# Linear attention ahead of a routed feed-forward layer: loads of k, v and q by head to 128 partitions, or by batch to 64

## The chip, the core and the metric

The kernel runs on one core of a Trainium2 chip. The metric is the time of one execution on the device, in microseconds (us). The kernel before has a median of 359.92 us in three runs (358.19 to 360.01). A profiled execution took 357.99 us, of which the profile shows a span of 355.7 us.

## The reference

Two layers follow each other. The first is attention without a softmax, over 8 batches, 8 heads, 576 rows and 64 numbers a row, in 32-bit floats:

```python
kv = np.einsum('bhsd,bhse->bhde', k, v)
out = np.einsum('bhsd,bhde->bhse', q, kv)
rms = np.sqrt(np.mean(out * out, axis=-1, keepdims=True) + 1e-06)
return (out / rms * g_norm).astype(np.float32)
```

So each head has one 64 x 64 matrix, k transposed times v, which needs every row of k and v; only then can a row of q be multiplied by it. The 8 heads of a row make 512 numbers, and 8 x 576 = 4608 such rows go to the second layer. It sends each row to the one of 8 experts with the largest gate value, through two matrices (512 x 1024 and 1024 x 512) with a ReLU between, and weights the result by the gate.

## The kernel before

**Attention.** The batches go in four pairs, P = 0 to 3. In an SBUF tile the first batch of a pair fills partitions 0 to 63, the second 64 to 127. Of the 576 rows of a head, the first 512 go to a main tile of 128 partitions x 8 heads x 512 numbers: partition p holds rows 8p to 8p + 7, so 8 x 64 numbers that lie together in memory, 2 KB. The last 64 rows go to a remainder tile (`load_rem`, L203), one row a partition. `load_main` (L211) brings a main tile, or some heads of it (`hs`), or some of the eight rows of each partition (`js`).

**What is loaded when.** `load_first` (L244) issues pair 0: k on SP's queue, v on ACT's, then q on SP's in two halves of `js`. All other loads are on SP's queue, in the order of the program: k, v and q of pair 1, k and v of pair 2 (L558), and then at fixed steps q of pair 2 (L506), k and v of pair 3 (L503), q of pair 3 (L507, in two halves), the weights of the first expert (L534) and of the second (L535, L536). k and v have two buffers each, for even pairs (kA, vA) and odd pairs (kB, vB, which lie in the slots of expert weights), and q has two. A load waits for its buffer's last reader. Completion is told by eight semaphores that the loads take in turn, so a load also waits for the one that had its semaphore before.

**What follows the loads.** `kv_mm` (L279) multiplies k and v of two heads for each call, four calls a pair; `kv_copy` (L297), `kv_t` and `kv_gate` prepare the result, with the gate's weights multiplied in. Then a loop of 36 steps (L574), nine for each pair, runs: a step s takes the j-th of the eight rows of every partition (or, for j = 8, the remainder tile). `heads` (L267) has POOL copy that row out of the main tile, four steps ahead; `x_qt` (L342) transposes it on PE, two steps ahead; `x_mm` (L352) multiplies; `x_norm` (L367) norms it on ACT and DVE. `Route` (L407) finds the expert and the place of each row, and `scatter` (L477) has POOL write the rows to a scratch tensor in DRAM, in the order of experts. The order on each engine is written by hand: lists `mid`, `late` and `last` (L488 to L536) say what stands behind which step. In POOL's order, the copy of `heads` for a step stands ahead of the ticks (L513, which pace POOL by DVE) and scatters of the step four earlier.

**The experts.** `gather` (L657) brings rows of one expert, five tiles of 128, with an indirect DMA from POOL; `flip` transposes them, `one` (L697) is the first matrix (L705) and ReLU (L712), `two` (L716) the second (L719), and L727 scatters the results to the output. Eight experts, and a ninth job for rows beyond 640 of an expert, follow each other. Weights come two experts ahead in 32 bits (L138, L146), to 128 partitions, and are cast (L168, L170, L175).

Of the kernel before, what the change touches and what calls it, by code (L numbers as in the profile page):

```python
# [28 lines left out]
def kernel(  # L29
# [154 lines left out]
    with (  # L184
# [6 lines left out]
        main, rem, qp, kvst, kvsb = {}, {}, {}, {}, {}  # L191
        srcs = {"k": k, "v": v, "q": q}
# [17 lines left out]

        def load_main(n, P, hs, js, eng):  # L211

            for bb in range(2):
                rows = srcs[n][2 * P + bb, hs, 0:512, :].rearrange("h (p j) d -> p h j d", j=8)
                dst = main[n, P][64 * bb:64 * bb + 64, hs, :].rearrange(
                    "p h (j d) -> p h j d", d=64
                )
                eng.dma_start(
                    dst[:, :, js, :].rearrange("p h j d -> p h (j d)"),
                    rows[:, :, js, :].rearrange("p h j d -> p h (j d)"),  # L220
                )

        ALL = slice(0, 8)
# [2 lines left out]
        def load_kv(P):  # L226
            for n in "kv":
                new_main(n, P)
                load_rem(n, P, nc.sync)
            for hs in HALF:  # L230
                for n in "kv":
                    load_main(n, P, hs, ALL, nc.sync)

        def load_q(P):
            new_main("q", P)
            if P == 3:
                load_main("q", P, ALL, HALF[0], nc.sync)
                load_rem("q", P, nc.sync)
                load_main("q", P, ALL, HALF[1], nc.sync)
            else:  # L240
                load_main("q", P, ALL, ALL, nc.sync)
                load_rem("q", P, nc.sync)
# [608 lines left out]
```

## Time and profile before

| What | Value |
|---|---|
| time, median of three | 359.92 us |
| span in the profile | 355.7 us |
| PE busy (matmul) | 271.1 us, 76% |
| DVE, ACT, POOL busy | 157.0, 159.0, 152.7 us |
| SP's queue (q1) | 39968 packets, 63.92 MB |
| indirect DMAs of POOL (q0) | 6976 packets, 18.96 MB |
| ACT's queue (q10) | 2880 packets, 2.38 MB |
| k, v, q main loads, size of one DMA | 512 or 1024 KB |

A row of slices cuts the span into 40 equal parts; a digit is the busy share in tenths. "GB/s" is what the core's 16 DMA engines moved in the slice. A row of waits reads: engine, tile and line that waited, what it waited for, then us in total, times, and the longest. A queue's row has packets, MB and the time that its packets took, as a share of 16 engines over the window that was asked; packets overlap in part, so a share can pass 100%. A row of the timeline starts with the time and the length of one or several equal instructions.

### The profile page before, as it was taken

What the parts mean: (1) busy time and instruction counts of PE and PEld (TensorE: products, weight loads), DVE (VectorE), ACT (ScalarE), POOL (GpSimd) and SP (SyncE); (2) the same over time, 40 slices, a digit from 0 to 9 for tenths busy, and PEclk for the clock granted to TensorE, in tenths of its full rate; (3) what the DMA queues carried; (4) which work ended last, traced back from release to release, by engine and by line L of the source; (5) the groups of instructions that cost most, each with busy time, mean ns of one, the idle gap of its engine ahead of it and who ended that gap; (6) DMA issues with size and microseconds to landing.
All of it is one profiled execution on the core that took longest, in us unless ns stands there. A gap on an engine that the chain in (4) does not pass through costs nothing. (4 is left out here: it accounts for less than half of the span.)

```text
span 355.7 us, 8916 instructions
## 1 busy us (share of the span) xinstructions
PE 271.1 (76%) x3684; PEld 180.5 (51%) x3684; DVE 157.0 (44%) x411; ACT 159.0 (45%) x338; POOL 152.7 (43%) x206
## 2 busy tenths in 40 slices
PE   7088725486653963676636999999999999999994
PEld 2056514474552753564412655656575747474742
DVE  0000532148612582448781239654545546363431
ACT  1001622156312552446577432737474747465652
POOL 8002200046216253256575753765555747413233
PEclk9678978779868597879658899999999999999998
DMA  7998999999999999994122792799798989896712
GB/s 150 223 218 185 200 228 226 214 210 249 254 217 221 258 246 293 377 381 169 67 99 74 254 361 81 274 308 398 237 400 260 363 284 383 262 394 202 282 61 83
DMA packets 49864, 85.82 MB, mean 241 GB/s; under 512 B 16797, under 2 KB 21150, under 8 KB 49824
## 3 DMA queue, kind: packets, MB, share of 16 engines
q1 hardware_dynamic: 39968, 63.92, 65.0%
q0 software_dynamic: 6976, 18.96, 15.1%
q10 hardware_dynamic: 2880, 2.38, 3.4%
q8 instruction: 29, 0.48, 0.6%
q14 instruction: 11, 0.09, 0.1%
HBM read 71.71 MB, written 15.50 MB: 245 GB/s over the span
## 5 line engine op out<-in xcount | busy, mean ns | idle before, releaser
L712 ACT ACTIVATE ht<-hp 128x320 f16<-128x320 f32 (+1 forms) x136 | 57.9, 428 | 71.5 <-PE hp L705 57.0
L705 PE MATMUL hp<-xt,we 128*128 128x320 f16 (+1 forms) x544 | 79.8, 295 | 0.0
L719 PE MATMUL yp<-we,ht 128*128 128x512 f16 x328 | 72.3, 379 | 0.0
L727 POOL DMA_INDIRECT out_dram<-ys,idx x41 | 42.6, 1038 | 64.9 <-DVE ys L724 56.6
L705 PEld LDWEIGHTS <-we 128*128 128x128 f16 x544 | 50.6, 98 | 19.1 <-issue 0.6
L361 PE MATMUL op<-kvs,qts 64*64 64x72 f32 x1152 | 34.8, 264 | 29.1 <-issue 18.7
L724 DVE TENSOR_SCALAR ys<-yp,xe 128x512 f32<-128x512 f32 x41 | 30.6, 750 | 47.1 <-PE yp L719 47.1
L719 PEld LDWEIGHTS <-ht 128*128 128x128 f16 x328 | 32.1, 98 | 37.1
L386 DVE TENSOR_REDUCE ms<-sq 128x8 f32<-128x512 f32 x36 | 24.5, 680 | 56.6 <-ACT sq L381 56.6
L275 POOL COPY qp<-qm 128x512 f32<-128x512 f32 x32 | 19.0, 614 | 70.5 <-DMA qm<-in_q_dram 70.5
L658 POOL DMA_INDIRECT xe<-xs_scratch,rowi x40 | 40.5, 1013 | 14.4 <-issue 9.6
L361 PEld LDWEIGHTS op<-kvs,qts 64*64 64x64 f32 x1152 | 28.7, 165 | 35.4 <-issue 20.6
L381 ACT ACTIVATE sq<-op 128x512 f32<-128x512 f32 x36 | 21.2, 590 | 47.7 <-PE op L361 47.6
L478 POOL DMA_INDIRECT xs_scratch<-xg,sli x36 | 35.3, 981 | 13.6 <-issue 12.8
L689 DVE COPY xt<-xp 128x512 f16<-128x512 f16 x41 | 17.4, 425 | 38.2 <-PE xp L686 37.9
L175 ACT CAST we<-ws 128x1024 f16<-128x1024 f32 x32 | 31.0, 1042 | 0.0
L292 PE MATMUL kvp<-vA,kA 64*64 64x64 f32 x512 | 14.0, 268 | 16.3 <-DMA vA<-in_v_dram 8.9
L350 ACT COPY qts<-qtp 128x512 f32<-128x512 f32 x36 | 21.0, 583 | 9.8 <-PE qtp L345 9.8
L292 PE MATMUL kvp<-vB,kB 64*64 64x64 f32 x512 | 13.4, 263 | 15.3 <-issue 8.4
L400 DVE TENSOR_TENSOR xg<-op,rinv 128x512 f16<-128x512 f32 x36 | 24.5, 682 | 0.0
L345 PE MATMUL qtp<-cf,qp 128*128 128x128 f32 x128 | 23.7, 314 | 1.0 <-ACT qts L350 0.4
L170 DVE TENSOR_SCALAR we<-ws,g 128x1024 f16<-128x1024 f32 x32 | 22.2, 757 | 0.0
(93 smaller groups left out, 241.9 us busy)
## 6 DMA issues: line engine op xcount, KB each, us to landing
ws<-in_moe_w_dram SPq DMA_DIRECT2D x16, 2048.0 KB, 11.7
kA<-in_k_dram SPq DMA_DIRECT2D x8, 512.0 KB, 13.6
qm<-in_q_dram SPq DMA_DIRECT2D x8, 512.0 KB, 10.4
kB<-in_k_dram SPq DMA_DIRECT2D x8, 512.0 KB, 10.5
vB<-in_v_dram SPq DMA_DIRECT2D x8, 512.0 KB, 18.1
qm<-in_q_dram SPq DMA_DIRECT2D x4, 1024.0 KB, 22.1
vA<-in_v_dram ACTq DMA_DIRECT2D x4, 512.0 KB, 14.2
vA<-in_v_dram SPq DMA_DIRECT2D x4, 512.0 KB, 17.9
```

Source lines behind the costliest of these rows:

```text
L175: nc.scalar.copy(self.w2[:, 2 * kk:2 * kk + 2, :], self.s2[:, 2 * kk:2 * kk + 2, :])
L292: nc.tensor.matmul(kvst[P][64 * hh:64 * hh + 64, bb, 64 * i:64 * i + 64], lhs, rhs, start=(j == 0), stop=(j == 8),)
L361: nc.tensor.matmul(op[cs, r, c0:c0 + 72], qts[s][rs, i, cs], kvs[rs, c, i // 2, n0:n0 + 72], start=True, stop=True,)
L386: nc.vector.reduce_sum(ms, sq, axis=AXX)
L400: nc.vector.tensor_tensor(xg[:, r, 0:512].rearrange("p (i h c n) -> p c i h n", c=2, i=2, h=2), ox, _bc(r4, 4, 64), op=ALU.mult,)
L478: nc.gpsimd.indirect_dma_start(out=xs_views[9 * self.P + self.g0 + t], out_offset=IndirectOffsetOnAxis(ap=self.sli[:, t:t + 1], axis=0), i ...
L658: nc.gpsimd.indirect_dma_start(out=xe.bitcast(I32), out_offset=None, in_=xs.ap(), in_offset=IndirectOffsetOnAxis(ap=rows, axis=0), bounds_ ...
L705: nc.tensor.matmul(hp, self.w.w1[:, kk, f * 128:(f + 1) * 128], self.xt[:, kk, ws * wd:(ws + 1) * wd], start=(kk == 0), stop=(kk == 3),)
L712: nc.scalar.activation(self.ht[:, f, ws * wd:(ws + 1) * wd], hp, ACTF.Relu)
L719: nc.tensor.matmul(yp, self.ht[:, f, t * 128:(t + 1) * 128], self.w.w2[:, f, :], start=(f == 0), stop=(f == 7),)
L724: nc.vector.tensor_scalar(ys, yp, self.xe[t][:, 514:516].bitcast(F32), None, op0=ALU.mult)
L727: nc.gpsimd.indirect_dma_start(out=self.views[t], out_offset=IndirectOffsetOnAxis(ap=self.idx[:, t:t + 1], axis=0), in_=ys, in_offset=None ...
```

## The change

Instead of one DMA for each batch of the pair, which covers all asked heads and writes 64 partitions, there is one for each head, which covers both batches and writes all 128 partitions. The piece that lies together in memory stays 2 KB (1 KB for the halves of q). The aim is that one transfer reaches all partitions of the destination. Remainders, constants and weights load as before, and so does all that follows the loads.

```diff
         def load_main(n, P, hs, js, eng):
 
-            for bb in range(2):
-                rows = srcs[n][2 * P + bb, hs, 0:512, :].rearrange("h (p j) d -> p h j d", j=8)
-                dst = main[n, P][64 * bb:64 * bb + 64, hs, :].rearrange(
-                    "p h (j d) -> p h j d", d=64
-                )
+            for h in range(8)[hs]:
+                rows = srcs[n][2 * P:2 * P + 2, h, 0:512, :].rearrange(
+                    "b (p j) d -> b p j d", j=8
+                )
                 eng.dma_start(
-                    dst[:, :, js, :].rearrange("p h j d -> p h (j d)"),
-                    rows[:, :, js, :].rearrange("p h j d -> p h (j d)"),
+                    main[n, P][:, h, 64 * js.start:64 * js.stop],
+                    rows[:, :, js, :].rearrange("b p j d -> b p (j d)"),
                 )
```

As instructions, a load of k before is source [64 rows of 2 KB, 4 heads, 512 numbers] to destination [64 partitions, 4 heads, 512 numbers]; after it is source [2 batches, 64 rows of 2 KB, 512 numbers] to destination [128 partitions, 512 numbers].

## The prediction

> **What bounds the kernel now.** I read the page's time slices first, then the queue's share in two short windows, then the waits, then the timeline around the last use of a loaded q. The slices:
>
> ```profile
> PE   7088725486653963676636999999999999999994
> DMA  7998999999999999994122792799798989896712
> GB/s 150 223 218 185 200 228 226 214 210 249 254 217 221 258 246 293 377 381 169 67 99 74 254 361 81 274 308 398 237 400 260 363 284 383 262 394 202 282 61 83
> ```
>
> A slice is 8.9 us. There are two stages. Up to slice 17 (about 155 us) the DMA engines are busy nine tenths and PE is not; yet they move only some 200 to 250 GB/s, while slices 16 and 17, in which the first expert's weights come, show 377 and 381. From 208 us on PE is full (the chain of waits runs through the matmuls L705 and L719). So the first stage is bound by loads that keep the DMA engines busy at little over half of what they move later. Two windows of the queue view (queue; packets, MB, share of 16 engines), 55 to 62 us with k, v and q in flight, then 157 to 160 us, mostly weights:
>
> ```profile
> q1 hardware_dynamic: 811, 1.59, 105.4%
> ```
>
> ```profile
> q1 hardware_dynamic: 501, 1.05, 89.9%
> ```
>
> First: 1.054 x 16 x 7 us = 118 engine-us for 811 packets, 146 ns a packet of (nearly all) 2 KB, 13.5 GB/s an engine. Second: 0.899 x 16 x 3 us = 43.2 engine-us for 501, 86 ns a packet of 2.1 KB on average, 24.3 GB/s an engine. Same size of packet, same engines; a weight tile has 128 partitions, a load of k has 64. Who waits for these loads:
>
> ```profile
> POOL qp L275 <- DMA qm<-in_q_dram: 70.5, 5, 30.8
> ACT kvs L300 <- DMA qm<-in_q_dram: 29.6, 1, 29.6
> PE kvp L292 <- DMA vA<-in_v_dram: 8.9, 3, 4.3
> PE kvp L292 <- DMA vB<-in_v_dram: 6.9, 2, 5.1
> ```
>
> Each step of attention hangs on the copy L275 out of q and, through kv_mm, on k and v.
>
> [...]
>
> **The change part by part.** *Destination.* It grows from 64 to 128 partitions[...]. Alone that would bring a packet from 146 to 86 ns.
>
> *Source.* It becomes `b p (j d)`: 2 batches, 64 rows, 512 numbers. The two batches lie 8 x 576 rows apart and the 64 rows span 512, so the first two dimensions can't be merged. The slowest dimension of the source is 2, that of the destination 128[...].
>
> *Bytes.* k, v and q without their last 64 rows are 3 x 64 heads x 512 rows x 256 B = 25.17 MB, 12.58 MB an engine. Price: the 24.3 GB/s that one engine reaches on 128 partitions[...]. 12.58 MB / 24.3 = 518 us. Bounds: [...]20 GB/s, should they keep part of the first window's slowness (13.5), 629 us.
>
> *Other traffic on these two engines before the last load.* The remainders (L206), unchanged: 24 DMAs x 512 packets / 16 = 768 packets of 256 B an engine. In 1 to 4 us, when only these run, q1 and q10 take 35.4% and 23.4% of 48 engine-us for 1396 packets, 20 ns each: 15 us. The scatters L478 of the first 27 steps: 27 x 128 rows x 1032 B / 16 = 0.22 MB, 9 us. First packet at about 2 us. Sum: 2 + 518 + 15 + 9 = 544 us until the last half of the last q has landed, against about 150 before.
>
> *Do the loads run without a gap?* The queue must not wait for a buffer. A third of a pair is 43 us (8 DMAs x 64 packets x 84 ns by bytes). k, v of pair 2 wait for kv_mm(0), done at about 90 us, and their turn is near 260; q of pair 2 waits for pair 0's copies, done near 140, turn near 350; k, v of pair 3 for kv_mm(1), near 220, turn near 390; the last q for pair 1's copies, near 280, turn near 480. No gap. A DMA waits for the one eight before it (eight completion semaphores): 8 x 5.4 = 43 us of work stays queued.
>
> *Issues.* load_main issues 44 DMAs before (12, 10, 10, 12 by pair) and 112 after (32, 24, 24, 32). The shortest issue takes 0.6 us; 68 more of them cost 41 us of SP and ACT, of 544, hidden by the transfers. ACT issues pair 0's v and then waits for slots, ahead of kv_copy(0), which needs that v anyway.
>
> *After the last load.* POOL's copies of pair 3 wait for q in two halves; the second half frees heads(31), the fifth of its eight copies. Before:
>
> ```profile
> 158.49 0.21 POOL L372 CAST xg<-cf 128x4 int32<-128x4 f32 x1
> 158.62 0.62 POOL L275 COPY qp<-qm 128x512 f32<-128x512 f32 x1
> ```
>
> From there to the end, 355.7 - 158.6 = 197 us; POOL's order of copies, ticks and scatters is fixed, so this stays, less some of the 5 us in which POOL there waits for L394: 195. The first four copies have the 22 us of the second half (8 x 64 packets of 1 KB at 42 ns, by bytes); before they took 24 (135.0 to 158.6), much of it waits for DVE, so POOL is at heads(31) by about then. The first two experts' weights queue behind q on the two engines: 4 x 2 MB / 16 = 0.52 MB an engine, 21.6 us, the first expert's after 11; they are needed 23 us (L168, at 181.7) and 26 us (L170, at 184.7) after heads(31). Hidden, by 12 and 4 us. Then the expert stage runs as before: its loads have 128 outermost, and PE is its bound.
>
> *Sum.* 544 + 195 = 739 us of span; runs stand 2 to 4 us above the span (357.99 in the profiled run, 359.92 median, for 355.7): 743.
>
> **The rivals.** *All 16 engines (faster).* If the source were regrouped to the destination's 128, or the engines counted from the destination alone, the loads would run at 24.3 GB/s an engine: 25.17 MB in 65 us and not 115. For: [...]the waits on q total 70.5 us. [...] Then POOL's row of work becomes the bound: copy 0.61, tick 0.19, scatter 0.98 and some 0.8 of issue, 2.6 us for each of 36 steps, 93 us, from about 25, with a tail of some 22 before the gathers: 140 and not 186. About 315 us.
>
> *Two engines, but in turn (faster).* If each DMA took the next pair of engines, eight in flight would fill 16. Landing of one is then 5.4 us and issue 0.6 us, so some nine overlap; with less even filling, about 330 us. [...]
>
> *Two engines, much slower.* If each engine, alone, needs the 146 ns of the first window: 12.58 MB / 13.5 = 932 us, in all about 1155. [...]
>
> *No change.* It needs a bound other than loads in the first stage; the waits speak against it.
>
> **How the numbers follow.** Two engines near the price taken: 0.82, 743 us. Two engines, outside the bounds: 0.05. All 16: 0.08. In turn: 0.04. No change: 0.01. The range holds the first case with its bounds: [...]above 629 + 26 + 195 = 850. The faster cases, near 320, stay outside. Slower 0.87, faster 0.12, same 0.01.
>
> **What would show it.** In the profile after: a stage of some 545 us with a DMA share of one to two tenths (2 of 16 engines) and near 49 GB/s; packets of 2 KB at about 84 ns; a landing time of 40 us or more for k, v and q; POOL's wait for qm in hundreds of us; the last 195 us as before. Two shares would fail the main step: nine tenths at 350 GB/s or more (all 16), or five tenths and above (in turn). A two-tenths share with packets well off 86 ns would fail only the price.

## The result, and the profile after

The changed kernel takes 727.17 us (median of four runs, 726.5 to 728.11), the kernel before 359.45 us beside it: a ratio of 2.0242, with a 95% interval of 2.0178 to 2.0305. The forecast was slower, 743 us, range 680 to 850. Where a kernel's runs differ by more than 1.5%, its slower runs are left out, here and below. Below the changed lines its line numbers are lower by one: L275 of before is L274, and so on.

The time slices of the changed kernel, 18.1 us each:

```profile
PE   3221034203110033221002523010455899999997
DMA  2111111311111132111113211111295749999971
GB/s 63 51 50 51 56 48 50 87 51 52 52 52 51 51 88 84 52 51 51 51 51 91 99 52 52 51 51 60 91 384 198 256 176 352 323 321 329 327 259 71
```

Up to slice 28 (525 us) the DMA engines are busy one tenth and move about 51 GB/s, where before it was nine tenths and 200 to 250. The slices above that (87, 88, 91) hold the remainders and the scatters, which still have all engines: they are nine tenths busy with remainders at 130 us, at up to 283 GB/s, and with a scatter at 270.7 us. With the first weights, in slice 29, the rate jumps to 384. Two windows of the queue view (queue: packets, MB, share of 16 engines); first 50 to 75 us, with k on SP's queue (q1) and v on ACT's (q10), then 150 to 200 us, with SP's alone:

```profile
q10 hardware_dynamic: 312, 0.63, 6.7%
q1 hardware_dynamic: 310, 0.63, 6.4%
```

```profile
q1 hardware_dynamic: 1260, 2.54, 13.1%
```

13.1% of 16 engines is 2.1 engines. With two queues in flight the sum is the same 13.1%, and the rate the same 51 GB/s: both use the same two. In the second window two engines move 2.54 MB in 50 us, 25.4 GB/s each. Where the time of the stage goes, in the waits (us in total, times, longest):

```profile
POOL qp L274 <- DMA qm<-in_q_dram: 228.4, 4, 104.1
...
POOL qp L274 <- DMA kr<-in_k_dram: 126.3, 1, 126.3
PE kvp L291 <- DMA vB<-in_v_dram: 111.4, 12, 23.5
PE kvp L291 <- DMA vA<-in_v_dram: 110.4, 13, 21.5
POOL qp L274 <- DMA qr<-in_q_dram: 108.9, 1, 108.9
```

POOL's copies wait 463.6 us for loads, 228.4 + 126.3 + 108.9, against 70.5 before. (The copy L274 reads only `qm`. kr and qr are named for two of its waits probably because loads share the eight semaphores, and a wait is put down to the transfer that came last.) Next the timeline of POOL around heads(31), the first copy out of the second half of the last q:

```profile
530.82 0.61 POOL L274 COPY qp<-qm 128x512 f32<-128x512 f32 x1 [15.17 <-DMA qm<-in_q_dram]
```

It starts at 530.8 us; before, at 158.6. From there on the two kernels are alike. The windows view (start and end, length, busy us of each engine, granted clock, DMA share, GB/s) of the rest, of the changed kernel and then of the kernel before:

```profile
531.00:725.00 194.00, 175.64 (x1291) 106.61 (x1291) 97.99 (x247) 106.03 (x204) 103.92 (x111) 0.92 0.76 270
```

```profile
158.60:355.70 197.10, 176.43 (x1365) 107.00 (x1357) 103.01 (x260) 108.85 (x213) 103.89 (x112) 0.93 0.69 242
```

PE's 176 us and POOL's 104 us are the same. PE's granted clock is low in the stage ahead of it (0.58 from 20 to 525 us, 0.81 from 20 to 140 us before), but PE is busy in only 105 of those 505 us, so it is not what holds the stage. So all the added time lies ahead of heads(31): 530.8 - 158.6 = 372 us, less 3 us of the rest, is the difference of the spans, 725.0 - 355.7 = 369.

### The profile page after: what moved, and what is told of

Read it like the earlier page. It is cut to its first block, busy times and chain, and to the rows that moved or that the text cites. A ratio compares the mean times of both kernels' runs of the same rounds, so it can differ in the third digit from the quotient of the medians.

```text
span 725.0 us, 9016 instructions
## 1 busy us (share of the span) xinstructions
PE 288.6 (40%) x3684; PEld 193.5 (27%) x3684; DVE 156.2 (22%) x411; ACT 159.5 (22%) x338; POOL 152.8 (21%) x206
## 5 line engine op out<-in xcount | busy, mean ns | idle before, releaser
L274 POOL COPY qp<-qm 128x512 f32<-128x512 f32 x32 | 19.1, 617 | 463.6 <-DMA qm<-in_q_dram 228.4
L344 PE MATMUL qtp<-cf,qp 128*128 128x128 f32 x128 | 26.9, 347 | 174.4 <-POOL qp L274 173.9
L291 PE MATMUL kvp<-vA,kA 64*64 64x64 f32 x512 | 18.9, 314 | 119.6 <-DMA vA<-in_v_dram 110.4
L344 PEld LDWEIGHTS qtp<-cf,qp 128*128 128x128 f32 x128 | 17.7, 174 | 178.2 <-POOL qp L274 175.3
L291 PE MATMUL kvp<-vB,kB 64*64 64x64 f32 x512 | 18.3, 313 | 111.4 <-DMA vB<-in_v_dram 111.4
L291 PEld LDWEIGHTS kvp<-vA,kA 64*64 64x64 f32 x512 | 16.6, 219 | 121.7 <-issue 77.9
L291 PEld LDWEIGHTS kvp<-vB,kB 64*64 64x64 f32 x512 | 16.1, 219 | 113.1 <-issue 61.2
L393 DVE TENSOR_TENSOR lr<-op,rinv 128x64 f32<-128x64 f32 x36 | 8.0, 222 | 175.5 <-ACT rinv L391 175.4
L360 PE MATMUL op<-kvs,qts 64*64 64x72 f32 x1152 | 37.4, 283 | 10.1 <-DVE xg L399 8.0
L360 PEld LDWEIGHTS op<-kvs,qts 64*64 64x64 f32 x1152 | 32.1, 183 | 16.0 <-DVE xg L399 11.3
```

Source lines behind the costliest of these rows:

```text
L291: nc.tensor.matmul(kvst[P][64 * hh:64 * hh + 64, bb, 64 * i:64 * i + 64], lhs, rhs, start=(j == 0), stop=(j == 8),)
L344: nc.tensor.transpose(qtp[:, i, :], qp[s][:, 2 * i:2 * i + 2, :], ident)
L360: nc.tensor.matmul(op[cs, r, c0:c0 + 72], qts[s][rs, i, cs], kvs[rs, c, i // 2, n0:n0 + 72], start=True, stop=True,)
```

## The experiments

The theory under test: the outermost sizes of a DMA's two sides set how many engines it gets, and 2 against 128 gives two. The prediction took this; no trace of the kernel before shows it, since its loads of k, v, q and weights have 64 or 128 outermost on both sides and its slices up to 155 us show the engines nine tenths busy. The rivals are that many small DMAs cost the time (112 issues in place of 44), and that one DMA with rows of both batches, which lie far apart in DRAM, reads slowly.

The first four runs (64, 4 and 8 outermost, and head by head on 64 partitions) were on a chip on which the kernel before takes 391.37 us (387.51 to 393.3): there the stretch after heads(31), which no load of k, v or q touches, takes 224 to 233 us and not 194 to 198. Why is open. I therefore compare the start of heads(31) for these, since all the loads of k, v and q lie ahead of it.

### Outermost size 64, 4 and 8 in place of 2

The first edit changes the order of two dimensions and nothing else:

```diff
-                    "b (p j) d -> b p j d", j=8
+                    "b (p j) d -> p b j d", j=8
...
-                    rows[:, :, js, :].rearrange("b p j d -> b p (j d)"),
+                    rows[:, :, js, :].rearrange("p b j d -> p b (j d)"),
```

> The changed kernel with one edit: the source's two outer dimensions change places (64 rows outside, 2 batches inside), same bytes, same number of DMAs, same 128 partitions. Partition 2p + b then holds what partition 64b + p should, so the rows of the two batches of a pair are mixed and the output's values are others; all work stays. Theory (the outermost sizes 2 and 128 leave two engines): now 64 and 128, 16 engines, packets of 2 KB stay at about 85 ns, the loads are done before 110 us and the time is 300 to 330 us. Rival (112 small DMAs, issued one by one, cost the time) and rival (rows of both batches in one DMA, far apart in DRAM, are slow to read): no gain over the changed kernel, about 725 us.

The next two keep the changed kernel's form, with more batches of fewer rows. With 4 batches (with 8, the numbers follow):

```diff
+            g, r = divmod(P, 2)
             for h in range(8)[hs]:
-                rows = srcs[n][2 * P:2 * P + 2, h, 0:512, :].rearrange(
+                rows = srcs[n][4 * g:4 * g + 4, h, 256 * r:256 * r + 256, :].rearrange(
```

> The changed kernel with 4 batches of 32 partitions in each DMA, in place of 2 of 64; bytes, number of DMAs and partitions stay. Batches are mixed within a tile, so the output's values are others; all work stays. Theory: outermost 4 and 128, four engines; 6.29 MB an engine at 25.2 GB/s is 250 us, with 26 us of other traffic 276, plus the 194 us after the last load of q: 470 us (450 to 490), DMA share near 0.26 and 100 GB/s in the loading stage. Both rivals: about 725 us, or more, since four batches lie further apart.

> As the run with four, but 8 batches of 16 partitions in each DMA (output's values are others; all work stays). Theory: eight engines, 3.15 MB each at 25.2 GB/s, 125 us, with 26 of other traffic about 150, plus 194: 345 us (335 to 370), DMA share near 0.5 and 200 GB/s. [...] Both rivals: 725 us or more.

Measured: 356.79 us with 64 outermost, 509.27 with 4 and 403.43 with 8 (one run of each of these two), beside 391.37 for the kernel before. All three lie above what was expected: 27 us above the range with 64, 39 above the 470 with 4, 58 above the 345 with 8. The slower stretch after heads(31) on this chip explains 30 to 39 us of it, and the stretch ahead of heads(31) the rest (283.3 us with 4 where 276 was expected, 167.8 with 8 where it was 150). The slices of the run with 4, then of that with 8:

```profile
DMA  3222252222433222433234992571567879679731
GB/s 97 102 106 101 96 133 101 104 102 102 119 121 135 102 102 107 131 143 120 103 110 147 353 395 88 177 291 43 208 224 289 303 266 361 200 300 316 252 150 72
```

```profile
DMA  5554755655565556997128602787497929697812
GB/s 140 200 195 155 176 205 206 188 172 213 219 191 178 216 216 184 364 402 280 68 75 315 225 28 88 277 283 277 136 398 215 375 101 347 241 311 266 300 54 75
```

51 GB/s at one tenth, 102 at two, about 205 at five: in these runs the rate follows the outermost size, some 25.5 GB/s an engine. In windows with almost nothing but pieces of 2 KB, SP's queue takes 13.1% of the 16 engines' time with 2 outermost (above), 26.2% with 4 (80 to 110 us) and 51.9% with 8 (46 to 58 us): 2.1, 4.2 and 8.3 engines. heads(31) starts, in POOL's timeline, with 4, 8 and 64 outermost:

```profile
283.31 0.61 POOL L275 COPY qp<-qm 128x512 f32<-128x512 f32 x1 [2.85 <-DMA qm<-in_q_dram]
```

```profile
167.82 0.61 POOL L275 COPY qp<-qm 128x512 f32<-128x512 f32 x1
```

```profile
133.50 0.61 POOL L274 COPY qp<-qm 128x512 f32<-128x512 f32 x1
```

With 2 it was 530.8. From 2 to 4 engines, half of 12.58 MB leaves each: 6.29 MB in 247.5 us is 25.4 GB/s, the rate of the window above. From 4 to 8, 3.15 MB in 115.5 us, 27.2 GB/s. From 8 to 16 it is 34.3 us where 1.57 MB at 25.4 would be 62. There the loads no longer wholly set the pace: with 64 outermost the copy heads(31) does not wait for a load, and from 20 to 110 us the engines move 278 GB/s at a share of 0.90, only some 19 GB/s for each busy engine. (The profiled execution with 64 outermost took 364.52 us; in that of its second try, below, heads(31) starts at 129.2.) Both rivals fall: number, size and bytes of the DMAs are the same in all four, and the rows of a DMA lie further apart with 4 and 8.

### The run with 64 outermost, once more

> The changed kernel with the 64 rows outside and the 2 batches inside once more (rows of the two batches of a pair mixed, so the output's values are others), beside the next run on one chip, since the first such run was on a chip on which the kernel before took 391 us. Theory: the loads are done near 110 us again, heads(31) starts at 125 to 134 us, and where the kernel before takes 359 us this takes 320 to 335. Rival (the gain was that chip's): within 8 us of the kernel before.

328.82 us (328.24 to 329.23) beside 357.08 for the kernel before (353.3 to 357.92), ratio 0.9257 (0.9135 to 0.9378). The kernel before varies more on this chip, but every run of it is at least 24 us above every run of this one. The same 112 DMAs to 128 partitions, but on 16 engines (a share of 0.92 and 283 GB/s from 20 to 110 us), are 24 to 30 us faster than before, so what the change aims at is real. Its slices, and POOL's heads(31), which waits for no load:

```profile
DMA  7967999999998899412249728997989999995612
GB/s 193 381 186 178 285 377 236 286 391 278 288 380 232 290 387 395 161 51 105 76 94 382 285 79 335 296 387 234 396 276 343 321 342 361 270 401 173 231 66 87
```

```profile
129.24 0.62 POOL L274 COPY qp<-qm 128x512 f32<-128x512 f32 x1
```

The rate alternates between 380 (k, v and q in pieces of 2 KB) and 180 to 290, where the 256-byte pieces of the remainders come and where q comes in halves, 128 KB an issue. The first 16 of these are issued in 12.2 us, one each 0.76 us, and from 16 to 24 us the engines are busy for only 0.68 of the time.

### Head by head, but 64 partitions

One part of the change alone, on the kernel before:

```diff
+            for h in range(8)[hs]:
+                for bb in range(2):
+                    rows = srcs[n][2 * P + bb, h, 0:512, :].rearrange("(p j) d -> p j d", j=8)
+                    eng.dma_start(
+                        main[n, P][64 * bb:64 * bb + 64, h, 64 * js.start:64 * js.stop],
+                        rows[:, js, :].rearrange("p j d -> p (j d)"),
+                    )
```

> The kernel before, with one part of the change alone: loads go head by head, but each batch of the pair keeps its own DMA to 64 partitions, the two batches in turn. 128 KB a DMA, twice the number of DMAs of the changed kernel, outermost 64 and 64. Theory: 16 engines; what limits is [...]0.6 us of issue for 128 KB (218 GB/s): 350 to 385 us. Rival (many small DMAs cost the time): above 725 us, since there are twice as many. [...]

402.53 us beside 391.37, ratio 1.0302 (1.0089 to 1.0515), on the chip with the slower expert stage; heads(31) starts at 174.1 us. That is about 370 us without the 30-odd us that this chip adds, within the 350 to 385 expected. Twice the changed kernel's number of DMAs costs 1 to 5%, not a factor of two. Its issues of k (min, median, max in ns) and, from the windows view, 120 to 150 us:

```profile
L216 SPq DMA_DIRECT2D kB<-in_k_dram x32: 467/595/1377, 48.4 to 139.5; - x32
```

```profile
120.00:150.00 30.00, 21.51 (x531) 17.11 (x532) 14.47 (x40) 13.10 (x34) 15.57 (x28) 0.78 0.79 219
```

One issue brings 131072 bytes (128 KB); in 595 ns that is 220 GB/s, and the window shows 219 at a DMA share of 0.79: here SP's issuing is the bound, and the engines have gaps.

### The changed loads for q alone

```diff
+            if n == "q":
+                for h in range(8)[hs]:
...
+                return
             for bb in range(2):
```

> The kernel before with the changed loads for q alone; k and v stay batch by batch on 64 partitions. Theory (two engines carry all of q, 16 engines the rest): each of the two has 4.19 MB of q at 25.2 GB/s, 166 us, plus its sixteenth of k and v, 1.05 MB at 13.5 to 25.2 GB/s, 42 to 78 us, plus 26 of other traffic: the second half of the last q is used at 235 to 270 us, and the time is that plus 194 (chip at the clock of the first runs) or 230 (chip of the runs before): 430 to 500 us. Rival (k and v in pieces by head are what delays; q is needed late and comes in time): within 20 us of the kernel before.

465.18 us (one run), beside 359.2. POOL's heads(31):

```profile
269.03 0.61 POOL L285 COPY qp<-qm 128x512 f32<-128x512 f32 x1 [14.65 <-DMA qm<-in_q_dram]
```

This is the upper end of what was expected: on each of the two engines q takes 166 us, its sixteenth of k and v 78 us at the 13.5 GB/s of the prediction's first window, and other traffic 26, together 270. The slices (11.6 us each) show how the time goes:

```profile
DMA  8931129811159611289222499268399989989632
```

Stretches of nine tenths (k, v) and of one (q) take turns. While q is under way on two engines, the other 14 stand nearly idle. That the queue's order and the limit of eight in flight make it so was not tried by itself. What the two engines have to do themselves already sums to the 269 us, so this run does not show that the idle time of the others adds to it.

### Halves in turn, 64 partitions

```diff
+            w = 2 if js.stop - js.start == 8 else 4
+            for h in range(8)[hs][::w]:
+                for bb in range(2):
...
+                        main[n, P][64 * bb:64 * bb + 64, h:h + w, 64 * js.start:64 * js.stop],
```

> The kernel before with its 64-partition DMAs cut to 256 KB (two heads; four for the halves of q) and the two batches in turn, outermost 64 and 64: 16 engines, and twice the bytes per issue of the head-by-head run on 64 partitions. If the engines, not in step with each other, write both halves of the partitions at once: 300 GB/s or more in the loading stage and 15 to 35 us less than the kernel before. [...]

349.45 us beside 359.2, ratio 0.9737 (0.9677 to 0.9798): 10 us, less than the 15 to 35 expected. heads(31) starts at 150.9 us, 7.7 earlier than before. From 20 to 140 us the engines move 249 GB/s, where the kernel before has this:

```profile
20.00:140.00 120.00, 73.58 (x1928) 58.59 (x1921) 47.75 (x132) 42.26 (x109) 35.01 (x64) 0.81 1.06 228
```

Both figures contain the scatters and, at the end, weights; up to 120 us they are 239 and 222. So the loads go some 8% faster, far from the 300 GB/s expected, which was the author's guess. Whether the 8% come from the halves in turn or from the smaller DMAs was not shown.

### A version with 16 engines and 128 partitions

The tile keeps its place but holds, in its first 256 columns, the first batch over all 128 partitions, four rows each, and in the others the second. Tokens' numbers follow, and the matmuls of k and v contract over 128 rows:

```diff
-            for bb in range(2):
-                rows = srcs[n][2 * P + bb, hs, 0:512, :].rearrange("h (p j) d -> p h j d", j=8)
...
+            for bb in range(8)[js][::4]:
+                bb = bb // 4
+                rows = srcs[n][2 * P + bb, hs, 0:512, :].rearrange("h (p j) d -> p h (j d)", j=4)
+                eng.dma_start(main[n, P][:, hs, 256 * bb:256 * bb + 256], rows)
...
-            for j in range(9):
+            for j in range(5):
...
-                            lhs, rhs = main["k", P][ps, h, c], main["v", P][ps, h, c]
+                            lhs, rhs = main["k", P][:, h, c], main["v", P][:, h, c]
...
-                            kvs[rs, c, i // 2, n0:n0 + 72], start=True, stop=True,
+                            kvs[rs, c if s % 9 == 8 else b0, i // 2, n0:n0 + 72],
+                            start=True, stop=True,
```

(`b0` is the batch of step s, `s % 9 // 4`.)

> A version that keeps 16 engines and reaches all 128 partitions: a DMA brings one batch to 128 partitions, four rows (1 KB) each, so both outermost sizes are 128; k and v of a batch are contracted over 128 partitions with four matmuls and the remainder in place of eight. Computes all of the reference. Theory: 1 KB packets at 46 ns, 22.3 GB/s an engine, 25.17 MB in 71 us, loads done near 115 us; then POOL's row of work bounds as in the run with the rows outermost: 25 to 40 us less than the kernel before. If 1 KB pieces or the new matmuls cost more than this: no gain over the kernel before.

310.75 us beside 359.2, ratio 0.8651 (0.8615 to 0.8687): 48 us faster than before, more than was expected, and the fastest of all here. From 60 to 75 us its engines move 341 GB/s at nine tenths, with most packets of 1 KB, where the expectation's 22.3 GB/s an engine make 357 (46 ns a packet is also what q of the changed kernel took from 126 to 128 us: 13.7% of 16 engines for 96 packets). Its slices, and POOL's heads(31):

```profile
DMA  7999999999999999422498189979899998978421
GB/s 171 350 311 224 358 351 209 348 361 280 294 369 312 404 398 401 150 97 73 120 386 300 68 325 297 403 228 377 328 302 336 284 397 270 353 291 257 170 104 61
```

```profile
111.71 0.61 POOL L270 COPY qp<-qm 128x512 f32<-128x512 f32 x1
```

47 us before the 158.6 of the kernel before; the stretch after it is 196.8 us, as before. To part the width in partitions from the matmuls, each of its DMAs was cut in two of 64 partitions:

```diff
-                eng.dma_start(main[n, P][:, hs, 256 * bb:256 * bb + 256], rows)
+                for ps in (slice(0, 64), slice(64, 128)):
+                    eng.dma_start(main[n, P][ps, hs, 256 * bb:256 * bb + 256], rows[ps, :, :])
```

> The version that brings one batch to 128 partitions, with each of its DMAs cut in two of 64 partitions each: half the matmuls of k and v as in that version, 16 engines, 1 KB pieces[...]. Computes all of the reference. [...] If they came from its fewer matmuls: 310 to 320 us.

342.76 us (341.48 to 344.71) beside 357.08 for the kernel before (353.3 to 357.92), ratio 0.9638 (0.9498 to 0.9778), some 13 us. The windows view of this version, 20 to 130 us, and of the one with 128 partitions, 20 to 100 us:

```profile
20.00:130.00 110.00, 78.30 (x1545) 61.24 (x1542) 48.39 (x133) 44.58 (x113) 32.62 (x60) 0.82 1.09 234
```

```profile
20.00:100.00 80.00, 65.55 (x1509) 51.80 (x1504) 49.02 (x134) 44.47 (x113) 33.78 (x63) 0.91 1.06 309
```

The 310 to 320 us expected of the fewer matmuls alone are not reached. In these two runs the full width of partitions is worth some 32 us (342.76 to 310.75, on two chips on which the kernel before is within 2 us; heads(31) comes 33.4 us earlier): with the engines as busy, they move 309 in place of 234 GB/s. The cut also halves the size of a DMA, but at a share of 1.09 the engines have no gaps in which they would wait for issues.

The other 13 us are there with 64 partitions too, and POOL's timelines show where. The kernel before, from heads(27), the first copy out of the last q (its copies heads(28) to (31) and shorter instructions left out):

```profile
135.04 0.61 POOL L275 COPY qp<-qm 128x512 f32<-128x512 f32 x1 [0.69 <-DMA qm<-in_q_dram]
...
144.77 0.19 POOL L513 COPY tick<-lr 128x1 f32<-128x1 f32 x1 [6.53 <-DVE lr L394]
...
150.67 0.19 POOL L513 COPY tick<-lr 128x1 f32<-128x1 f32 x1 [3.62 <-DVE lr L394]
...
156.83 0.18 POOL L513 COPY tick<-lr 128x1 f32<-128x1 f32 x1 [2.56 <-DVE lr L394]
```

The version with 64 partitions, to heads(31):

```profile
132.42 0.61 POOL L271 COPY qp<-qm 128x512 f32<-128x512 f32 x1 [8.45 <-DMA qm<-in_q_dram]
...
137.87 0.19 POOL L511 COPY tick<-lr 128x1 f32<-128x1 f32 x1 [1.05 <-DVE lr L392]
...
143.34 0.18 POOL L511 COPY tick<-lr 128x1 f32<-128x1 f32 x1 [1.86 <-DVE lr L392]
...
145.13 0.61 POOL L271 COPY qp<-qm 128x512 f32<-128x512 f32 x1
```

At heads(27) it leads by 2.6 us, at heads(31) by 13.5 (145.1 against 158.6). So most of the 13 us is not in the loads: it lies between these two copies, where POOL waits 2.9 us for DVE in place of 12.7. In that stretch PE runs 164 of the last pair's 288 matmuls of k and v in the kernel before, and 56 of 160 here; it also has gaps there which the profile puts down to nothing that it shows, 10.4 us before and 2.5 here. That the fewer matmuls make the difference fits this, but was not tried alone.

## Why the prediction was right

**What bounds.** That the first stage is bound by loads at little over half of the rate that the engines reach later stood: with 128 partitions and 16 engines, two versions gain 24 to 30 and 48 us. Why a load to 64 partitions is the slower one, no trace shows: what was measured is 13.5 GB/s an engine with it and 24.3 with weights to 128, and 234 against 309 GB/s in the two versions of one batch. Of the 47 us by which heads(31) comes earlier in the second, 13.5 do not come from the width in partitions. The loads of k, v and q end somewhat earlier in the kernel before than the 150 us of the prediction: from 138 to 143 us the engines already move 351 GB/s, as with weights, and heads(31) at 158.6 waits for no load.

**Two engines.** The step that decides held, though no trace of the kernel before had shown it: with 2, 4 and 8 outermost the loads ran on 2.1, 4.2 and 8.3 engines, at 51, 102 and 205 GB/s. Both queues use the same two: 6.7% and 6.4%, where SP's alone takes 13.1%.

**The price.** 24.3 GB/s an engine was mis-sized by some 4%: it measured 25.4 with pieces of 2 KB. The lower end of the range, 680 us, rested on a higher rate that no trace had shown. The forecast's 518 us for 12.58 MB would be 495 at that rate. heads(31) started at 530.8 and not 544, so 13 of these 23 us show; the other 10 went to terms that were put too low. The 1 KB pieces of two pairs' q, which ran at 49 GB/s and not 51 (126 to 128 us, both engines), make some 3 us of them: 4.19 MB at 49 is 86 us and not 82. The rest I did not part. So the sum came out a little better than its largest term, since two errors of opposite sign partly cancelled.

**No gap.** SP's timeline, 144.9 to 207.4 us, with groups of four DMAs to a buffer:

```profile
144.91 20.77 SPq L217 DMA_DIRECT2D vB<-in_v_dram  x4
165.72 20.74 SPq L217 DMA_DIRECT2D kB<-in_k_dram  x4
186.51 20.92 SPq L217 DMA_DIRECT2D vB<-in_v_dram  x4
```

20.8 us for four is 5.2 a DMA, the time of 64 packets on each engine at 81 ns: SP issues at the pace at which DMAs land. The turns came near the forecast: k and v of pair 2 from 264 us (260 forecast), q of pair 2 at 338 (350), k and v of pair 3 at 394 (390), the last q at 469 (480). In the whole stage the rate never falls below 48 GB/s in a slice, so no wait for a buffer is seen.

**After the last load.** 195 us forecast, 194.2 measured (725.0 - 530.8). The first expert's weights are cast (L168) at 551.2 us, 20.4 us after heads(31), and nothing waits for them, as forecast. The landing times that the forecast named could not be read, since the profile gives none for these DMAs; the issue times above stand in for them.

**The sum.** 739 us of span forecast, 725.0 measured: 13 from the loads, 1 from the rest. The rivals with 16 engines put the loads at 65 us and the time near 315. The run with 64 outermost, which has 16 engines, gives 328.82, so that estimate was some 14 us too low. It took the full rate for all of k, v and q, where the halves of q came at 180 to 290 GB/s, and 2.6 us for each of POOL's steps, without waits for DVE, of which POOL has 8 us in two steps from 115 to 128 us. How the 14 us divide was not measured.

## What to carry to other kernels

Before a load is widened to all partitions, read the outermost size of both of its sides: here a batch index of 2 in front of the rows left the loads on two of sixteen DMA engines (51 GB/s), although the destination has 128 partitions. If the layout needs such an index outside, try another layout, so that one DMA has one batch over all 128 partitions with rows outermost; here that made a factor of two slower into 13% faster. In these profiles the mark was a DMA share that stayed flat through the stage (0.13, 0.26 and 0.52 for 2, 4 and 8), with a rate for each busy engine of 24 to 26 GB/s, as high as the 24.3 of the weights. A low share alone is not enough: head by head on 64 partitions it was 0.79 with 16 engines, since SP could not issue faster (595 ns for each 128 KB).

## What the runs showed that was not expected

Loads on two engines took turns with those on 16: with q alone on two engines, stretches in which all 16 engines carry k and v (nine tenths busy) stood between stretches in which only two worked (one tenth, 48 GB/s from 225 to 237 us). The stage took 269 us, which is what q (166 us), a sixteenth of k and v (78) and other traffic (26) cost on each of those two engines; the other 14 stood nearly idle in the stretches of q. And an arrangement that was meant only as a way to 16 engines brought some 13 us that the width in partitions does not explain. Most of them lie behind the loads, in a stretch in which POOL waits for DVE (12.7 us before, 2.9 with the new arrangement).
